# Attention's small matmuls as four 64x64 tiles: operands without zero blocks, two exponentials per pair of heads

## The chip, the cores and the metric

The kernel runs on one core of one Trainium2 chip. A core has a matrix engine (TensorE; PE in the profile, its weight loads PEld), a vector engine (VectorE, DVE), a scalar engine (ScalarE, ACT), GpSimd (POOL) and SyncE (SP), which work side by side and wait for one another through semaphores. POOL and SP also issue most transfers. The metric is the device time of one execution in microseconds, lower is better. Three timed executions of the kernel before gave 365.85 us as their median, from 364.59 to 366.14.

## The reference

Windowed attention with a few global positions, followed by a wide layer with an activation and a second matrix product:

```python
def _attn_ref(q, k, v, global_idx):          # B, H, S, D = 8, 8, 576, 64; 8 global positions
    window = 32
    scores = scale * np.matmul(q, k.transpose(0, 1, 3, 2))
    mask = np.abs(pos[:, None] - pos[None, :]) <= window
    mask = mask | is_global[:, None] | is_global[None, :]
    scores = np.where(mask, scores, -1000000000.0)
    scores = scores - np.max(scores, axis=-1, keepdims=True)
    attn = np.exp(scores)
    attn = attn / (np.sum(attn, axis=-1, keepdims=True) + 1e-09)
    return np.matmul(attn, v).astype(np.float32)

def _moe_ref(x, w_in, w_out, alpha):         # x: 4608 x 512; w_in: 512 x 2048; w_out: 2048 x 512
    h = x @ w_in
    s = np.sin(alpha * h)
    g = h + s * s / (alpha + 1e-09)
    return (g @ w_out).astype(np.float32)
```

## The kernel before

**Attention, one pair of heads at a time.** A batch has eight heads, worked as four pairs (`hp` 0 to 3; the two heads of a pair are `t` 0 and 1). The 576 keys of a head are split into 12 tiles of 48 (`NT12`); each key tile is joined by the 8 global keys. Two key tiles of even and odd number (`i % 2`) hold the even and odd positions of one segment. A key tile meets only 60 columns of even and 60 of odd queries, its window and the global queries, so one score matmul has 120 columns (`WCOL`).

Keys lie in `KX` so that head 0 of a pair has partitions 0 to 63 and columns 0 to 63 of a 128x128 block, head 1 the rest, and the two other 64x64 blocks are zero. One 128x128 matmul per key tile (L742) gives both heads' scores at once: 12 a pair, four into one PSUM tile of the ring `ring` (two buffers), then one exponential on ACT (L750) and one multiplication by `MASK` on DVE (L753) for these four: three of each a pair. Values `VX` have the same block form, and `OB` is a block matrix of ones, which sums the exponentials. `products` (L784) multiplies each key tile's `E` by `VX` (numerator) and by `OB` (denominator); the output columns are split into two halves at `CUT`, each a PSUM bank, and two of the 12 tiles cross the cut: 14 matmuls each, 28 a pair, of 120, 88 or 32 columns. They add up in `zn` (numerator) and `zd` (denominator), two banks each; the last pair has its numerator in `zd` and its denominator in the banks of `zr`, which the ring gives up. Then ACT takes the logarithm of the denominator and the exponential of its negative (L810, L813, the reciprocal), DVE sums the global queries' columns (L794) and multiplies (L816) into `xT`, the input of the wide layer.

**The order of work is written by hand.** `attention` issues, for each pair, the scores of this pair, then the products of the pair before, then reciprocal and normalisation of the pair before. Between them `fill(n)` issues the next n matmuls of `gemm2` of the batch before: the second matrix product, 128x128 by 512 columns (L1049), in blocks of 16 that add up in one of two banks `zo[0]`, `zo[1]`, taken in turn; ACT copies each finished block out (L1055) and SP stores it (L1062). A `gemm2` has four blocks (even batches) or five (odd ones), 64 or 80 matmuls. How many go where is given by START, PER_SCORES, MIDST and, within `gemm1`, PER_GROUP; LATE and GROUP_LATE hold for the first batches.

**gemm1** (L992) makes the hidden layer: 16 groups of 8 matmuls of 288 columns into `zn`, `zr`, `zd` in turn, then Sin on ACT (L1022), the square on ACT or DVE (L1026, L1028) and the sum on DVE into `H2` (L1030). Then the attention of the next batch runs beside `gemm2` of this one. `beside` puts DVE copies of the next keys and queries (L350, L357) between.

**Loads.** POOL issues the value loads (`load_v`, 16 a batch) and writes the global keys and queries (`place_globals`); SP issues the global values (`load_vg`, 8 a batch), the transposes of keys and queries (`turn_qk`) and the stores. At the start `KX`, `QX` and `VX` are cleared by ACT, DVE and POOL. The lines behind L1193 run 54 matmuls on the values and `H2` whose results nobody reads, in 64x64 tiles and whole.

Of the kernel before, what the change touches and what calls it, by code (L numbers as in the profile page):

```python
# [10 lines left out]
ALU = mybir.AluOpType  # L11
AF = mybir.ActivationFunctionType
DT = mybir.dt
# [234 lines left out]
def kernel(  # L248
# [43 lines left out]
    VX = [main.tile([P, NHP, NT12, P], DT.bfloat16, name=f"VX{i}") for i in range(2)]  # L292
    KX = [main.tile([P, NHP, NT12, P], DT.bfloat16, name=f"KX{i}") for i in range(2)]
# [7 lines left out]
    OB = main.tile([P, P], DT.bfloat16, name="OB")  # L301
    MASK = main.tile([P, NT12, WCOL], DT.bfloat16, name="MASK")
# [10 lines left out]
    W2 = main.tile([P, DFF], DT.bfloat16, name="W2")  # L313
    limit = main.tile([P, 1], DT.float32, name="limit")
    EA = main.tile([P, B * NHP * 3], DT.float32, name="EA")
# [29 lines left out]
    def place(b, which, t, y, copy, hps=slice(0, NHP)):  # L345
# [10 lines left out]
        else:  # L356
            copy(  # L357
                out=KX[b % 2][rows, hps, :, t * D + y * 24 : t * D + y * 24 + 24],
# [8 lines left out]
    def place_globals(b):  # L367

        for hp in range(NHP):
            for t in range(2):  # L370
                rows = slice(t * D, (t + 1) * D)
                nc.gpsimd.tensor_copy(
                    out=KX[b % 2][rows, hp, :, t * D + KT : t * D + KT + NG],
                    in_=kTg[rows, hp, None, :, b].to_broadcast([D, NT12, NG]),
                )
# [13 lines left out]
    def load_v(b, hps=range(NHP)):  # L389
        for hp in hps:  # L390
            for t in range(2):
                for y in range(2):
                    r = t * D + y * 24
                    nc.gpsimd.dma_start(  # L394
                        out=VX[b % 2][r : r + 24, hp, :, t * D : t * D + D],
                        in_=v[b, 2 * hp + t].rearrange("(i a y) d -> y a i d", a=24, y=2)[y],
                    )

    def load_vg(b):
        for h in range(H):  # L400
            t = h % 2
            src = VGb[b::B, h * D : (h + 1) * D] if b else VG0[h::H]
            nc.sync.dma_start(
                out=VX[b % 2][t * D + KT : t * D + KT + NG, h // 2, :, t * D : t * D + D],
                in_=src[:, None, :].to_broadcast([NG, NT12, D]),
            )
# [28 lines left out]
    zn, zd = [banks.tile([P, 2, 512], DT.float32, name=name) for name in ("zn", "zd")]  # L435
    zo = [banks.tile([P, 512], DT.float32, name=f"zo{i}") for i in range(2)]

# [800 lines left out]
```

## Time and profile before

| what | value |
|---|---|
| median of three timed runs | 365.85 us |
| profiled execution, its own time | 366.15 us |
| its span, first to last instruction | 364.4 us |
| mean granted TensorE clock | 0.993 of full |
| attention of batch 0, first scores to first matmul of gemm1 | 16.14 to 33.60 us |
| attention of batch 1 | 54.42 to 72.07 us |
| attention of batch 2 | 96.96 to 115.68 us |
| gemm1 of batch 2 (with the START matmuls behind it) | 115.68 to 136.34 us |
| attention of batch 3, gemm1 of batch 3 | 136.34 to 155.06 to 175.35 us |
| gemm1 of batch 7 begins | 311.10 us |

In a profile page "busy" is the time in which an engine has at least one instruction at work; a matmul's duration includes its way through the array, so successive matmuls overlap, and their pace is read from the distance of their starts. "Idle before, releaser" tells how long an engine stood before an instruction and which event let it go on. The costliest groups of the page and some of its waits:

```profile
L1049 PE MATMUL zo<-w_out,H 128*128 128x512 bf16 x576 | 153.7, 379 | 0.0
L750 ACT ACTIVATE E<-ring 128x480 bf16<-128x480 f32 x96 | 54.2, 567 | 22.6 <-PE ring L742 22.2
L753 DVE TENSOR_TENSOR E<-E,MASK 128x480 bf16<-128x480 bf16 x96 | 36.0, 405 | 16.9 <-ACT E L750 15.5
L742 PE MATMUL ring<-QX,KX 128*128 128x120 bf16 x384 | 38.0, 225 | 6.5 <-ACT E L750 3.0
```

Each line is a group: source line, engine, operation, tiles out<-in, shapes and count, then busy microseconds and mean nanoseconds of one, then the engine's idle time before it and what ended it.

### The profile page before, as it was taken

How to read it: one execution, taken by the hardware profiler on the slowest of the kernel's cores; microseconds unless marked ns; L12 is line 12 of the kernel's file. 1: busy time of each engine (PE TensorE's matmuls, PEld its weight loads, DVE VectorE, ACT ScalarE, POOL GpSimd, SP SyncE). 2: the span in 40 equal slices, each digit the busy share in tenths (PEclk: the TensorE clock that was granted, in tenths of full speed). 3: DMA queues.
4: the chain of work that ended last, by engine and by line, in shares of the span. 5: the costliest groups of instructions: out<-in, count | busy, mean ns of one | idle time of the engine just before them, and what ended most of it. 6: DMA issues, size and time to landing. Idle time of an engine off the chain costs nothing. (4 is left out here: it accounts for less than half of the span.)

```text
span 364.4 us, 8575 instructions
## 1 busy us (share of the span) xinstructions
PE 338.4 (93%) x3110; PEld 230.8 (63%) x3110; DVE 283.3 (78%) x623; ACT 293.5 (81%) x566; POOL 139.2 (38%) x246
## 2 busy tenths in 40 slices
PE   2579978999999999999999999999999999999994
PEld 1467656766567666776666766766676766655453
DVE  6776998588988877888888887888788866798661
ACT  7689997886978788887888897979888888878711
POOL 7992686669874702661066304730000000000001
PEclk9999998999999999999999999999999999999999
DMA  7997999999999783989199904647120011000321
GB/s 118 120 171 162 181 146 189 156 168 198 146 237 202 73 123 81 172 89 161 31 158 120 149 29 50 68 50 148 43 59 29 2 31 60 29 3 0 105 70 53
DMA packets 103580, 38.07 MB, mean 104 GB/s; under 512 B 94139, under 2 KB 98251, under 8 KB 103083
## 3 DMA queue, kind: packets, MB, share of 16 engines
q0 software_dynamic: 56640, 18.56, 44.6%
q1 hardware_dynamic: 46890, 18.89, 25.5%
q8 instruction: 26, 0.43, 0.5%
q14 instruction: 24, 0.19, 0.2%
HBM read 37.15 MB, written 17.83 MB: 151 GB/s over the span
## 5 line engine op out<-in xcount | busy, mean ns | idle before, releaser
L1049 PE MATMUL zo<-w_out,H 128*128 128x512 bf16 x576 | 153.7, 379 | 0.0
L992 PEld LDWEIGHTS <-w_in 128*128 128x128 bf16 x1024 | 98.6, 98 | 45.6 <-issue 9.1
L394 POOL DMA_DIRECT2D VX<-in_v_dram x128 | 83.3, 659 | 89.8 <-PE zd L784 62.9
L1049 PEld LDWEIGHTS <-H 128*128 128x128 bf16 x576 | 52.3, 97 | 37.2
L750 ACT ACTIVATE E<-ring 128x480 bf16<-128x480 f32 x96 | 54.2, 567 | 22.6 <-PE ring L742 22.2
L753 DVE TENSOR_TENSOR E<-E,MASK 128x480 bf16<-128x480 bf16 x96 | 36.0, 405 | 16.9 <-ACT E L750 15.5
L1083 POOL DMA_INDIRECT out_dram<-osb,ghalf x1 | 1.1, 1067 | 119.6 <-POOLq L1206 119.6
L1030 DVE SCALAR_TENSOR_TENSOR H<-s,recipT,zn 128x576 bf16<-128x576 bf16 x47 | 38.2, 814 | 10.3 <-ACT s L1026 6.5
L1026 ACT ACTIVATE s<-sb 128x576 bf16<-128x576 bf16 (+1 forms) x62 | 42.7, 689 | 2.0
L742 PE MATMUL ring<-QX,KX 128*128 128x120 bf16 x384 | 38.0, 225 | 6.5 <-ACT E L750 3.0
L742 PEld LDWEIGHTS <-KX 128*128 128x128 bf16 x384 | 29.0, 102 | 22.0 <-issue 8.8
L1022 ACT ACTIVATE sb<-zn,alphaT 128x576 bf16<-128x576 f32 (+1 forms) x47 | 34.7, 739 | 9.8 <-PE zn L992 9.7
L1030 DVE SCALAR_TENSOR_TENSOR H<-s,recipT,zd 128x576 bf16<-128x576 bf16 x39 | 31.7, 814 | 6.5 <-ACT s L1026 4.7
L1030 DVE SCALAR_TENSOR_TENSOR H<-s,recipT,zr 128x576 bf16<-128x576 bf16 x39 | 31.7, 813 | 4.5 <-ACT s L1026 2.4
L1022 ACT ACTIVATE sb<-zd,alphaT 128x576 bf16<-128x576 f32 (+1 forms) x39 | 28.9, 740 | 7.1 <-PE zd L992 5.8
L1028 DVE TENSOR_TENSOR s<-sb 128x576 bf16<-128x576 bf16 (+1 forms) x66 | 30.7, 465 | 4.1 <-ACT sb L1022 3.6
L1022 ACT ACTIVATE sb<-zr,alphaT 128x576 bf16<-128x576 f32 (+1 forms) x39 | 28.9, 740 | 5.6 <-PE zr L992 5.4
L784 PEld LDWEIGHTS <-VX 128*128 128x128 bf16 x448 | 26.6, 100 | 9.4 <-issue 3.5
L1055 ACT COPY osb<-zo 128x512 f32<-128x512 f32 x36 | 20.8, 577 | 11.3 <-PE zo L1049 10.0
L992 PE MATMUL zn<-xlast,w_in 128*128 128x288 bf16 (+1 forms) x192 | 28.8, 289 | 0.3
L992 PE MATMUL zn<-xT,w_in 128*128 128x288 bf16 x184 | 26.9, 286 | 2.3 <-DVE H L1030 0.9
L784 PE MATMUL zn<-E,VX 128*128 128x120 bf16 (+2 forms) x336 | 26.9, 211 | 1.0 <-DVE xlast L816 0.9
(163 smaller groups left out, 492.6 us busy)
## 6 DMA issues: line engine op xcount, KB each, us to landing
VX<-in_v_dram POOLq DMA_DIRECT2D x128, 36.0 KB, 5.4
kd<-in_k_dram POOLq DMA_DIRECT2D x7, 576.0 KB, 7.1
qd<-in_q_dram POOLq DMA_DIRECT2D x7, 576.0 KB, 10.1
w_in<-in_moe_w_in_dram POOLq DMA_DIRECT2D x4, 512.0 KB, 6.0
w_out<-in_moe_w_out_dram POOLq DMA_DIRECT2D x4, 512.0 KB, 7.8
out_dram<-osb SPq DMA_DIRECT2D x8, 256.0 KB
out_dram<-osb SPq DMA_DIRECT2D x8, 224.0 KB
out_dram<-osb SPq DMA_DIRECT2D x8, 192.0 KB
```

The costliest lines, as they stand in the source:

```text
L394: nc.gpsimd.dma_start(out=VX[b % 2][r : r + 24, hp, :, t * D : t * D + D], in_=v[b, 2 * hp + t].rearrange("(i a y) d -> y a i d", a=24, y= ...
L742: nc.tensor.matmul(out=ps[:, e * WCOL : (e + 1) * WCOL], lhsT=kx[:, hp, i, :], rhs=qx[:, hp, :, s0 : s0 + 60], start=True, stop=True, skip ...
L750: nc.scalar.activation(out=Eg, in_=ps[:, 0 : 4 * WCOL], func=AF.Exp, scale=scale, accum_out=EA[:, n : n + 1])
L753: nc.vector.tensor_tensor(out=Eg, in0=Eg, in1=MASK[:, 4 * g : 4 * g + 4, :].rearrange("p i c -> p (i c)"), op=ALU.mult,)
L784: nc.tensor.matmul(out=out_t[:, half, :, a - half * CUT : z - half * CUT], lhsT=OB[:] if key else VXb[:, hp, i, :], rhs=E[:, i, :, a - s0 ...
L992: nc.tensor.matmul(out=h[e][:, 0:W], lhsT=lhsT, rhs=xT[:, c, e, 0:W], start=(c == 0), stop=(c == CT - 1), skip_group_check=True,)
L1022: nc.scalar.activation(out=sb[:, es, 0:W], in_=h[:, :, 0:W], func=AF.Sin, scale=alphaT[:, nt : nt + 1])
L1026: nc.scalar.activation(out=s2[:, :, 0:W], in_=sb[:, :, 0:W], func=AF.Square)
L1028: nc.vector.tensor_tensor(out=s2[:, :, 0:W], in0=sb[:, :, 0:W], in1=sb[:, :, 0:W], op=ALU.mult)
L1030: nc.vector.scalar_tensor_tensor(out=H2[:, nt, r0 : r0 + S].rearrange("p (e c) -> p e c", e=2)[:, es], in0=s2[:, es, 0:HALF], scalar=recip ...
L1049: nc.tensor.matmul(out=ops[:], lhsT=H2[:, nt, blk * P : (blk + 1) * P], rhs=w_out[:, nt, :], start=(nt == 0), stop=(nt == NT - 1),)
L1055: nc.scalar.copy(out=osb[:], in_=ops[:])
```

## The change

Keys, values, the exponentials `E` and the mask lose their zero blocks. A key tile is now 64 columns wide with the two heads on the two halves of the partitions; `E` and the mask hold even key tiles on partitions 0 to 63 and odd ones on 64 to 127; `OB` goes, and 64 columns of `ones` take its place. Every matmul of the attention works on 64 rows and 64 columns: for scores, the head picks the rows of the array and the parity of the key tile its columns; for products, the parity picks the rows and the head the columns. There are twice as many matmuls, 24 for scores and 56 for products a pair, issued in rounds over the four tiles.

The two row halves are kept in different PSUM banks. Products therefore run in two parts, `crossed` 0 and 1, with `nc.tensor.drain()` between. The scores of a pair go, 8 key tiles of each head, into the two banks of `zr` (now a fixed tile), with one exponential over 960 columns; the remaining third, four of 120 columns, goes into one bank, `zd` for pair 0 and otherwise a `zo` bank that `pick()` chooses, written half before and half after the drain, with a second exponential over 480 columns. `gemm2` also takes its banks from `pick()`. All scores of a pair, its `fill` in one stretch and all products of the pair before now follow one another; the matmul counts for `fill` are 3 at the start, 14 a pair, 4, and 9 within gemm1. `load_vg` issues 12 loads a batch, `place_globals` writes four key pieces instead of eight, the clearing of `KX` and `VX` halves, and the unread matmuls at the end go. Set-up code for mask and places follows the new layout (not shown).

```diff
-    VX = [main.tile([P, NHP, NT12, P], DT.bfloat16, name=f"VX{i}") for i in range(2)]
-    KX = [main.tile([P, NHP, NT12, P], DT.bfloat16, name=f"KX{i}") for i in range(2)]
+    VX = [main.tile([P, NHP, 2, NT12 // 2, D], DT.bfloat16, name=f"VX{i}") for i in range(2)]
+    KX = [main.tile([P, NHP, NT12, D], DT.bfloat16, name=f"KX{i}") for i in range(2)]
...
+    zr = banks.tile([P, 2, 512], DT.float32, name="zr")
     zo = [banks.tile([P, 512], DT.float32, name=f"zo{i}") for i in range(2)]
+    used, opened, clock = [0, 0], [], [0]
+
+    def pick():
+        return min((i for i in range(2) if i not in opened), key=lambda i: used[i])
+
+    def use(i):
+        clock[0] += 1
+        used[i] = clock[0]
+        return zo[i]
...
+        def slot(t, g, u):
+            return 8 + 2 * t + u if g == 2 else 4 * t + 2 * g + u
+
+        def score(hp, g, u, t, z, c):
+            for r in range(2):
+                i = 2 * (g + 3 * u) + r
+                s0 = PAD + begin(i)
+                nc.tensor.matmul(
+                    out=z[r * D : (r + 1) * D, c * WCOL : (c + 1) * WCOL],
+                    lhsT=kx[t * D : (t + 1) * D, hp, i, :],
+                    rhs=qx[t * D : (t + 1) * D, hp, :, s0 : s0 + 60],
+                    start=True, stop=True, skip_group_check=True,
+                )
+
+        def scores(hp):
+            Es[hp] = pairp.tile([P, NT12, WCOL], DT.bfloat16, name="E")
+            for c in range(4):
+                for t in range(2):
+                    score(hp, c // 2, c % 2, t, zr[:, t, :], c)
+
+        def scores_last(hp, t, z):
+            for u in range(2):
+                score(hp, 2, u, t, z, 2 * t + u)
+
+        def expo(hp, n, z):
+            at = (b * NHP + hp) * 2 + n
             nc.scalar.activation(
-                out=Eg, in_=ps[:, 0 : 4 * WCOL], func=AF.Exp, scale=scale, accum_out=EA[:, n : n + 1]
-            )
+                out=Es[hp][:, 8:] if n else Es[hp][:, 0:8].rearrange("p (t i) c -> p t (i c)", t=2),
+                in_=z[:, 0 : 4 * WCOL].rearrange("p (i c) -> p i c", c=WCOL) if n else z[:, :, 0 : 4 * WCOL],
+                func=AF.Exp, scale=scale, accum_out=EA[:, at : at + 1],
+            )
...
+        def product(hp, key, g, crossed):
+            out_t = nd(hp, key)
+            for u in range(2):
+                for r in range(2):
+                    half = r ^ crossed
+                    v = u ^ half
+                    i = 2 * (g + 3 * v) + r
+                    if half not in parts_of(i):
+                        continue
+                    a, z = parts_of(i)[half]
+                    s0 = begin(i)
+                    rows = slice(r * D, (r + 1) * D)
+                    for t in range(2):
+                        bank = (hp, key, half, t)
+                        E = Es[hp][rows, slot(t, g, v)].rearrange("p (x c) -> p x c", x=2)
+                        nc.tensor.matmul(
+                            out=out_t[t * D : (t + 1) * D, half, :, a - half * CUT : z - half * CUT],
+                            lhsT=ones[rows, 0:D] if key else VXb[rows, hp, t, g + 3 * v, :],
+                            rhs=E[:, :, a - s0 : z - s0],
+                            start=bank not in begun, stop=True, skip_group_check=True,
+                        )
+                        begun.add(bank)
+
+        def products(hp, crossed):
+            for key in (1, 0):
+                for g in range(3):
+                    product(hp, key, g, crossed)
...
+        def scores_products(hp, third):
+            scores_last(hp, 0, third)
+            if hp:
+                products(hp - 1, 0)
+            nc.tensor.drain()
+            scores_last(hp, 1, third)
+            if hp:
+                products(hp - 1, 1)
...
+            n_start, n_fill = (START, PER_PAIR) if b > 1 else (0, LATE)
+            fill(n_start)
+            beside(-1)
+            for hp in range(NHP):
+                third = use(pick())[:] if hp else zd[:, 0, :]
+                scores(hp)
+                scores_products(hp, third)
+                expo(hp, 0, zr)
+                mask(hp, 0)
+                if hp:
+                    invert(hp - 1)
+                expo(hp, 1, third)
+                if hp:
+                    normalise(hp - 1)
+                mask(hp, 1)
                 if wide and hp == last:
                     keep_globals(slice(0, last))
+                fill(n_fill[hp])
+                if b == 1 and hp < 2:
+                    idle()
+                beside(hp)
+        products(last, 0)
+        nc.tensor.drain()
+        products(last, 1)
         inverse(last)
         nc.scalar.preload_act_table(AF.Sin)
         sums(last, 1)
         fill(MIDST)
-        products(last, range(3), (0,))
         sums(last, 0)
...
     def gemm2(b):
         lo, hi = (0, 4) if b % 2 == 0 else (4, 9)
         for blk in range(lo, hi):
-            ops = zo[(blk + b // 2) % 2]
+            z = pick()
+            opened.append(z)
+            ops = use(z)
             for nt in range(NT):
...
             nc.scalar.copy(out=osb[:], in_=ops[:])
+            opened.clear()
+            use(z)
...
-    START = 2
-    PER_SCORES = ((1, 11, 3), (3, 3, 4), (3, 3, 4), (3, 4, 5))
-
-    LATE = ((0, 0, 0), (0, 0, 0), (2, 3, 3), (4, 4, 6))
+    START = 3
+    PER_PAIR = (14, 14, 14, 14)
+
+    LATE = (0, 0, 8, 14)
     MIDST = 4
-    PER_GROUP = (0, 0, 5) + 11 * (1,) + (0, 0)
+    PER_GROUP = (0, 0, 5, 0, 1, 0, 0, 1, 0, 0, 1, 0, 1, 0, 0, 0)
```

`inverse` is the logarithm and the exponential of its negative; `invert(hp)` is `inverse` and the two `sums`. For batch 0 a separate order without `fill` uses `zd`, `zr` and the two `zo` banks in turn for the last third.

236 lines of the change are left out of this document (99 added, 137 removed).

## The prediction

> **What bounds the kernel now.** I read the page first, then the engines' busy time stretch by stretch, then the timeline of one attention stage and of the last microseconds, and the list of waits. The profiled execution took 366.15 us, its span 364.4 us, so 1.75 us lie around the span; the median of the runs shown is 365.85 us, 0.3 us below. The sum is made against 366.15 and 0.3 is taken off at the end.
>
> ```profile
> span 364.4 us, 8575 instructions
> PE 338.4 (93%) x3110; PEld 230.8 (63%) x3110; DVE 283.3 (78%) x623; ACT 293.5 (81%) x566; POOL 139.2 (38%) x246
> ```
>
> An average says little about stages, so here are one attention stage (136 to 155 us) and the first matrix product after it (155 to 175 us); the columns are the stretch, its length, then the busy time of PE, PEld, DVE, ACT and POOL.
>
> ```profile
> 136.34:155.06 18.72, 18.71 (x213) 12.51 (x213) 15.07 (x35) 16.20 (x41) 8.12 (x13) 1.00 0.72 128
> 155.06:175.35 20.29, 20.02 (x150) 14.21 (x148) 16.89 (x29) 16.94 (x27) 6.93 (x15) 1.00 0.91 111
> ```
>
> The reader is to see that PE is idle for 0.01 us of the one and 0.27 us of the other, at a granted clock of 1.00, while ACT and DVE have 2 to 4 us to spare. Six such cycles (attention of batches 2 to 7 with the first products behind them) run at about 39 us each. In them only TensorE's own time and new waits of TensorE count; fewer exponentials are worth nothing while matmuls hide ACT (without that cover one of 0.55 us a pair would go, less what the longer one takes more).
>
> **What one pair of heads costs now.** The timeline of that stage:
>
> ```profile
> 136.98 2.53 PE L1049 MATMUL zo<-w_out,H 128*128 128x512 bf16 x11
> ...
> 141.93 0.36 PE L784 MATMUL zn<-E,VX 128*128 128x88 bf16 x4
> ...
> 142.79 0.37 PE L742 MATMUL ring<-QX,KX 128*128 128x120 bf16 x4
> ...
> 143.00 0.36 PE L784 MATMUL zn<-E,VX 128*128 128x120 bf16 x4
> ...
> 143.39 1.03 PE L1049 MATMUL zo<-w_out,H 128*128 128x512 bf16 x4
> 143.66 0.19 ACT L750 ACTIVATION_READ_ACCUMULATOR E<-ring 128x1 f32 x1
> 143.76 0.73 ACT L810 ACTIVATE L<-zd,tiny 128x576 f32<-128x576 f32 x1
> ```
>
> Starts tell pace. Four score matmuls take 143.00-142.79 = 0.21 us, 0.0525 each. The 28 products of a pair take (142.79-141.93)+(143.39-143.00) = 1.25 us. A pair is 3x0.21+1.25 = 1.88 us, a stage 4x1.88 = 7.52 us. A second-product matmul takes (2.53-0.38)/10 = 0.215 us, 0.38 being the length of a lone one; its 72 a cycle do not change.
>
> **What tiles cost.** The kernel before ends with matmuls in 64x64 tiles (L1199), so the trace prices them:
>
> ```profile
> 354.28 1.46 PE L1049 MATMUL zo<-w_out,H 128*128 128x512 bf16 x6
> 355.66 1.06 PE L1076 MATMUL zo<-w_out,HG 128*64 128x256 bf16 x16
> ...
> 357.91 0.54 PE L1199 MATMUL zd<-H,VX 64*64 64x120 bf16 x24
> 358.24 0.79 PE L1199 MATMUL zn<-H,VX 64*64 64x120 bf16 x24
> 358.96 0.49 PE L1199 MATMUL zd<-H,VX 128*128 128x120 bf16 x6
> ```
>
> The first 24 go round all four tiles: six rounds in 358.24-357.91 = 0.33 us, 0.055 a round with the start, so four tiles do cost what one whole matmul costs (0.0525). A change between whole array and tiles: the last 512-column matmul starts at 354.28+5x0.215 = 355.36 and would make room at 355.57, and the next kind starts at 355.66: 0.09 us. The next 24 go two by two, twelve rounds in 358.96-358.24-0.09 = 0.63, 0.0525 each again.
>
> Now the changed stage, from the diff. Scores: a pair has four rounds of four tiles into zr and, for the third part, two rounds of two tiles on each side of the drain: 8x0.0525 = 0.42, a stage 1.68. Products: for each of numerator and denominator a tile gets four matmuls before the drain and three after, of 120, 88 or 32 columns. No tile matmul in the trace is narrower than 120; if width counted, as it does in the whole array (1.25 us for 28), a pair is 0.60, if each is a full round 14x0.0525 = 0.735. I take 0.735, the row with tiles: 2.94 a stage. The Trainium skill (TensorEngine Tiling (Array Packing), Restrictions) has column tiles lose the fast weight load; the trace has 107 ns for a 64-wide load against 98 for a whole one, and by the rule the 0.735 would hold, by width 0.5 us a stage less. Changes of mode: two a pair and two for the last pair's products, 10x0.09 = 0.9. Drains: five a stage, and none stands in this stage of the trace. Below, a drain is an emptied array, 0.09. Above, it is the last matmul's 0.21, a weight load of 0.10, and the 28 matmuls behind it at 0.028 each (54 loads of L1199 in 1.52 us) in place of eight rounds, 0.78-0.42 = 0.36: 0.67. I take 0.30, the last matmul's end and the load, since a drain waits for the one and keeps the other from being fetched ahead: 1.5. Sum 1.68+2.94+0.9+1.5 = 7.02, so tiles gain 0.5 us a stage, 3.0 in six.
>
> **Waits that the change adds.** (a) The third part of the scores now goes to whichever zo bank the second product has not open, and the next block of the second product, 16 matmuls long, takes just that bank, because pick() returns the one used longest ago. That block then stands behind the pair's second exponential, which is queued on ACT behind logarithm and reciprocal of the pair before. From the products' last start: 0.1 to the logarithm, 0.76 to the next,
>
> ```profile
> 144.52 0.68 ACT L813 ACTIVATE R<-L 128x576 f32<-128x576 f32 x1
> ...
> 145.20 0.55 ACT L750 ACTIVATE E<-ring 128x480 bf16<-128x480 f32 x1
> ```
>
> 0.68 to the exponential, 0.57 for it: 2.1 us. The fill of 14 starts 0.14 after the products; a block that begins after its matmul number o waits 2.1-0.14-0.215o. Counting START 3, 14 a pair, MIDST 4, 9 in the first product against blocks of 16: with 80 matmuls to place (attention of batches 2, 4, 6) blocks begin at o=13 of pair 0, 1 of pair 2 and 3 of pair 3; with 64 (3, 5, 7) at 5 of pair 0, 7 of pair 1, 9 of pair 2, 11 of pair 3. Pair 0 uses zd, so nothing there waits for an exponential. Waits 1.75+1.32 and 0.45+0.02. After o=13 the bank's copy (0.58) is also late for the third part of pair 1: its block's last matmul lands 0.96 with the copy after its start, PE is there at 2x0.215+0.09+0.21 = 0.73, 0.23. Together 3.3 and 0.47, for three of each 11.3 us. PE works in order, so scores, products and the fill behind it all move. (b) Pair 0's third part goes to zd, where group 14 of the first product lies until
>
> ```profile
> 136.46 0.81 DVE L1030 SCALAR_TENSOR_TENSOR H<-s,recipT,zd 128x576 bf16<-128x576 bf16 x1 [0.29 <-ACT s L1026]
> ```
>
> 137.27. After the last first-product matmul (the fill starts at 135.91) PE needs 3x0.215+0.09+0.21 and would be there at 136.86: 0.41. Seven fewer fill matmuls in that stage let DVE and ACT trail it more; I take 0.6, bounds 0 and 1: 3.6 in six.
>
> **Parts at nothing.** Batch 0 and 1 wait for chains on ACT and DVE: fewer exponentials (four of 0.55 a batch) against masks and products that now wait for a longer exponential with no fill; 0, bounds -1.5 and +1.5. Setup is shorter by one clearing of 1.34 on DVE and part of the mask, but the queries' copies on DVE hold the first scores, -0.3 inside that bound. Four KX copies fewer on POOL before batch 1 would start its scores 1.6 earlier, but the table load ends at 55.12 and the first exponential starts at 55.14 already. SP gets 12 loads of global values a batch for 8, which took 5.76 us in the setup (0.72 each): 2.9 us more on its queue, ahead of the turning of the next keys and the stores; they are issued before a first product of 20 us, which covers it. POOL's value loads stay 16 a batch. The probe L1199 runs beside the last output's transfer and is worth nothing.
>
> **Sum.** -3.0+11.3+3.6 = +11.9: 366.15+11.9 = 378.05, less 0.3: 378.
>
> **Rivals.** *Cheap drains and no bank waits (faster):* place, pairs 1 to 3; the second exponential is done before the block needs its bank, that is within 0.36 us of the products in pair 2. For it: ACT has 2.5 us to spare in the stage. Against it: the order of ACT's queue. Then 11.3 goes; a drain of 0.09 gives 6x1.05 = 6.3 and narrow products 6x0.5 = 3.0: 357. Without bank waits it turns from slower to faster once a drain is under 0.28. *No bank waits, drains as taken:* 366.5. *Issue sets the pace:* tiles double the attention matmuls to 80 a pair; at 0.028 each 2.24 instead of 1.155, 4.3 a stage, 26 in all: 404. For it: 54 loads in 1.52 us, never tried for longer; against it, rounds of 0.0525 are four at 0.013. The Trainium skill (TensorE: Matmul & The Clock Gate, "Wait — 56ns, not 53.3ns?") has the sequencer spend about 62 ns on a matmul with hardware decoding off; an estimate by it is 4.96 us a pair and some 470 us. The trace starts 48 tile matmuls in 1.05 us, 22 ns each, which speaks against it as far as so short a run can. *Tiles do not run side by side:* 80x0.0525 a pair, 73 us more, 451; the rounds of L1199 speak against it.
>
> **Chances.** Forecast 0.60, own range 370 to 389 (drains 0.09 to 0.67 are -6.3 and +11, half the bank waits -5.6). Faster rival 0.17, no bank waits 0.12, issue 0.08, one by one 0.03. Within 0.5%, which is 364.0 to 367.7, is what a measurement cannot tell from no change: 0.07 of the third case and 0.01 of others, so 0.08; faster 0.19, slower 0.73. Range 358 to 391: it leaves out half of the faster rival and the two slow ones.
>
> **What would show it.** Right: idle of TensorE before the second product's first matmul of a block, released by the exponential, near 1.7 us in pair 2 of the 80s; idle before the third part of pair 0 released by DVE's H; gaps of about 0.35 from start to start at drains; rounds of 0.0525. Wrong: blocks that begin without idle, drains under 0.15, or stretches of tiles slower than four in 0.06.

## The result, and the profile after

The changed kernel takes 404.6 us (median of four runs, 402.5 to 408.2), the kernel before beside it 366.0 us: a ratio of 1.1075, with a 95% interval from 1.0985 to 1.1164. Slower was forecast; the 378 us and the range up to 391 were too low. The profiled execution is the longest of the four, 408.2 us. Its page begins so:

```profile
span 406.5 us, 10957 instructions
PE 341.2 (84%) x4330; PEld 208.9 (51%) x4330; DVE 279.6 (69%) x586; ACT 288.4 (71%) x502; POOL 123.2 (30%) x219
```

TensorE's busy time hardly moved (338.4 us before), its share fell from 93 to 84%: it now waits. Between the starts of the stages (first scores of a batch to its first matmul of gemm1, and on to the next scores) the 42 us lie here:

| stretch of the profiled execution | before | after | more |
|---|---|---|---|
| start to first scores of batch 2 | 97.0 | 111.4 | 14.4 |
| attention of batch 2 and gemm1 of batch 2 | 39.4 | 51.0 | 11.6 |
| attention of batch 3 to attention of batch 7 | 174.8 | 192.4 | 17.6 |
| gemm1 of batch 7 to the end | 53.3 | 51.8 | -1.5 |

Below: attention of batch 3, gemm1 of batch 3, attention and gemm1 of batch 4, with the columns of the same view before (stretch, length, busy PE, PEld, DVE, ACT, POOL).

```profile
162.32:183.17 20.85, 19.74 (x382) 10.52 (x382) 14.56 (x31) 15.35 (x33) 9.03 (x15) 1.00 0.77 117
183.17:203.70 20.53, 19.51 (x142) 13.53 (x140) 17.13 (x31) 17.39 (x26) 4.29 (x10) 1.00 0.52 86
203.70:227.47 23.77, 19.96 (x382) 10.64 (x382) 14.55 (x31) 15.29 (x33) 11.06 (x21) 1.00 0.76 114
227.47:248.00 20.53, 19.50 (x141) 13.53 (x139) 17.22 (x31) 17.88 (x27) 2.08 (x4) 1.00 0.49 84
```

Attention grew from 18.72 to 20.85 us (batch 3) and from 18.7 to 23.77 (batch 4). gemm1 did not shrink (20.29 before), though six matmuls of the second product had been moved out of it and TensorE is idle for a whole microsecond of it. The timeline of TensorE in the attention of batch 4:

```profile
203.70 0.40 PE L757 MATMUL zr<-QX,KX 64*64 64x120 bf16 x16
204.25 0.67 PE L757 MATMUL zd<-QX,KX 64*64 64x120 bf16 x8
204.85 3.19 PE L1126 MATMUL zo<-w_out,H 128*128 128x512 bf16 x14
...
212.92 0.40 PE L757 MATMUL zr<-QX,KX 64*64 64x120 bf16 x16
...
213.42 0.35 PE L828 MATMUL zn<-E,VX 64*64 64x120 bf16 x16
213.89 0.24 PE L757 MATMUL zo<-QX,KX 64*64 64x120 bf16 x2
...
214.41 0.39 PE L1126 MATMUL zo<-w_out,H 128*128 128x512 bf16 x1
216.51 2.97 PE L1126 MATMUL zo<-w_out,H 128*128 128x512 bf16 x13 [1.72 <-ACT E L779]
...
220.90 0.82 PE L1126 MATMUL zo<-w_out,H 128*128 128x512 bf16 x3
223.01 2.53 PE L1126 MATMUL zo<-w_out,H 128*128 128x512 bf16 x11 [1.29 <-ACT E L779]
```

The small matmuls of a whole pair, scores and products, go from 212.92 to 214.41: 1.49 us, where the same work took 1.88. The last product before the drain starts at 213.59, the first matmul behind it at 213.89: 0.30 from start to start. Then, one matmul and three matmuls into the fill, TensorE stands for 1.72 and 1.29 us before a new block of the second product: the bank waits of the prediction (1.75 and 1.32), at the predicted matmuls.

The first row of the table, and some 6 us of the second (an even batch is about 5 us longer in any case), have other reasons. SP's queue and GpSimd at the start, before:

```profile
15.88 5.76 SPq L403 DMA_DIRECT2D VX<-VG  x8
32.26 2.16 SPq L340 DMA_TRANSPOSE kt<-kd  x1
36.46 0.33 POOL L1127 COPY seen<-kt 1x1 bf16<-1x1 bf16 x1 [6.90 <-DMA kt<-kd]
49.92 0.63 POOL L696 CAST VGb<-H 64x512 bf16<-64x512 f32 x1
```

and after:

```profile
15.88 11.23 SPq L404 DMA_DIRECT2D VX<-VG  x16
38.09 2.04 SPq L340 DMA_TRANSPOSE kt<-kd  x1
42.37 0.18 POOL L1206 COPY seen<-kt 1x1 bf16<-1x1 bf16 x1 [13.78 <-DMA kt<-kd]
55.53 0.67 POOL L710 CAST VGb<-H 64x512 bf16<-64x512 f32 x1
```

Batch 0 has sixteen loads of global values for eight (each head twice, once for each half of the partitions). They hold up the queries and then the key transposes on SP by 5.8 us. GpSimd waits for those transposes in its own order (a one-element copy stands ahead of its next loads), so w_in, the values of batch 1, w_out and the table `VGb` all come 5.6 us later. And in the attention of batch 2, from the timeline of all engines, in order of time:

```profile
105.97 0.53 POOL L331 DMA_DIRECT2D kd<-in_k_dram  x1
106.26 10.36 SPq L340 DMA_TRANSPOSE kt<-kd  x1
116.73 5.81 SPq L340 DMA_TRANSPOSE qt<-qd  x1
122.73 0.92 DVE L357 COPY KX<-kt 64x1152 bf16<-64x1152 bf16 x2 [6.67 <-DMA kt<-kd]
124.53 0.31 PE L828 MATMUL zd<-E,ones 64*64 64x88 bf16 x10 [3.78 <-DVE GS L844]
```

The transposes of batch 3's keys and queries start together with the casts of batch 4 (L331, DRAM to DRAM) and take 10.4 and 5.8 us, where before they took 4.4 and 3.9 and had ended when those casts were issued (101.33 us). DVE's placing of these keys stands ahead of the masks of this batch, so the products wait.

### The profile page after: what moved, and what is told of

Read it like the earlier page. It is cut to its first block, busy times and chain, and to the rows that moved or that the text cites. A ratio compares the mean times of both kernels' runs of the same rounds, so it can differ in the third digit from the quotient of the medians.

```text
span 406.5 us, 10957 instructions
## 1 busy us (share of the span) xinstructions
PE 341.2 (84%) x4330; PEld 208.9 (51%) x4330; DVE 279.6 (69%) x586; ACT 288.4 (71%) x502; POOL 123.2 (30%) x219
## 3 DMA queue, kind: packets, MB, share of 16 engines
q1 hardware_dynamic: 47178, 18.89, 22.7%
## 5 line engine op out<-in xcount | busy, mean ns | idle before, releaser
L1126 PE MATMUL zo<-w_out,H 128*128 128x512 bf16 x576 | 143.9, 386 | 10.2 <-ACT E L779 10.2
L1126 PEld LDWEIGHTS <-H 128*128 128x128 bf16 x576 | 54.3, 99 | 69.8 <-issue 17.6
L788 DVE TENSOR_TENSOR E<-E,MASK 128x960 bf16<-128x960 bf16 x64 | 33.2, 529 | 33.0 <-ACT E L779 32.5
L779 ACT ACTIVATE E<-zr 128x960 bf16<-128x960 f32 (+1 forms) x33 | 31.6, 957 | 31.7 <-PE zr L757 31.7
L757 PEld LDWEIGHTS <-KX 64*64 64x64 bf16 x768 | 18.3, 112 | 31.6 <-issue 30.8
L1132 ACT COPY osb<-zo 128x512 f32<-128x512 f32 x36 | 20.9, 580 | 11.6 <-PE zo L1126 9.1
L828 PE MATMUL zd<-E,ones 64*64 64x120 bf16 (+2 forms) x672 | 23.8, 224 | 6.4 <-DVE GS L844 3.8
L828 PE MATMUL zn<-E,VX 64*64 64x120 bf16 (+2 forms) x672 | 22.3, 224 | 7.5 <-DMA VX<-VGb 4.5
L860 ACT ACTIVATE L<-zd,tiny 128x576 f32<-128x576 f32 x24 | 17.8, 741 | 14.2 <-PE zd L828 13.7
```

Source lines behind the costliest of these rows:

```text
L757: nc.tensor.matmul(out=z[r * D : (r + 1) * D, c * WCOL : (c + 1) * WCOL], lhsT=kx[t * D : (t + 1) * D, hp, i, :], rhs=qx[t * D : (t + 1) * ...
L779: nc.scalar.activation(out=Es[hp][:, 8:] if n else Es[hp][:, 0:8].rearrange("p (t i) c -> p t (i c)", t=2), in_=z[:, 0 : 4 * WCOL].rearran ...
L788: nc.vector.tensor_tensor(out=Em, in0=Em, in1=MASK[:, 2 * n : 2 * n + m // 2].rearrange("p g u c -> p (g u c)")[:, None].to_broadcast([P, ...
L828: nc.tensor.matmul(out=out_t[t * D : (t + 1) * D, half, :, a - half * CUT : z - half * CUT], lhsT=ones[rows, 0:D] if key else VXb[rows, hp ...
L1126: nc.tensor.matmul(out=ops[:], lhsT=H2[:, nt, blk * P : (blk + 1) * P], rhs=w_out[:, nt, :], start=(nt == 0), stop=(nt == NT - 1),)
L1132: nc.scalar.copy(out=osb[:], in_=ops[:])
```

## Experiments

Each was run beside the kernel before (366.2 to 366.7 us). "A2 at" is the first score of batch 2 in the profiled execution, "A2" the length of its attention, "A3-A7" the stretch of the table above.

| kernel | us, median | ratio to before, 95% | A2 at | A2 | A3-A7 |
|---|---|---|---|---|---|
| before | 366.0 | | 97.0 | 18.7 | 174.8 |
| the change | 404.6 | 1.1075 (1.0985 to 1.1164) | 111.4 | 30.4 | 192.4 |
| second exponential first | 396.5 | 1.0815 (1.0672 to 1.0958) | 112.3 | 25.9 | 185.8 |
| the same, and old spread in gemm1 | 390.6 | 1.0655 (1.0594 to 1.0715) | 112.1 | 20.5 | 182.1 |
| no global value loads | 399.3 and 420.6 | | 102.2 | 50.8 | 192.5 |
| global values by rows, batch 1 on | 400.3 | 1.0918 (1.0886 to 1.0950) | 109.4 | 23.5 | 192.7 |
| late casts | 406.2 | 1.1087 (1.1053 to 1.1120) | 111.7 | 25.0 | 193.9 |
| before, casts early | 368.0 and 388.5 | | 96.5 | 40.0 | 175.0 |
| all four, batch 0 by rows behind the queries | 389.4 | 1.0638 (1.0595 to 1.0680) | 112.8 | 19.3 | 182.5 |
| the same, first third in zo | 404.3 | 1.1034 (1.0987 to 1.1082) | 113.9 | 24.2 | 190.7 |
| all four, batch 0 as in the change | 390.9 | 1.0656 (1.0619 to 1.0693) | 110.0 | 22.7 | 183.1 |
| the same, START 4 | 389.0 | 1.0634 (1.0565 to 1.0703) | 109.3 | 20.2 | 180.5 |
| as two rows above, 32 more drains | 395.4 | 1.0789 (1.0746 to 1.0832) | 112.0 | 21.1 | 187.0 |
| START 4, 22 more idle matmuls | 387.4 | 1.0551 (1.0506 to 1.0595) | 113.1 | 19.0 | 180.0 |
| the change, batch 0 by rows, early | 401.6 | 1.0964 (1.0918 to 1.1010) | 106.6 | 26.2 | 194.7 |
| START 4 and batch 0 by rows, early | 380.7 | 1.0396 (1.0355 to 1.0438) | 106.7 | 18.8 | 180.7 |

### The cycles

*The second exponential ahead of the logarithm.*

```diff
+                expo(hp, 1, third)
                 if hp:
                     invert(hp - 1)
-                expo(hp, 1, third)
-                if hp:
                     normalise(hp - 1)
```

> Only the order on ACT changes, for batches from 1: the second exponential is issued ahead of the logarithm and the reciprocal of the pair before. Theory: the waits of TensorE before a new block of the second product (1.72 and 1.29 us in pairs 2 and 3 of batch 4) are that exponential, queued 1.45 us behind the other two; it is now done about 0.5 us after the products, so the waits fall under 0.4 us, some 2.5 us an even batch and 0.4 an odd one: about 396 us. Rival: the block waits for something else that ends at the same time (the copy out of the bank, or the masks of the pair): no change, 403 us or more.

TensorE's waits from the attention of batch 3 to the end of that of batch 7, total, times and longest, in the change:

```profile
PE zo L1126 <- ACT E L779: 7.3, 7, 1.7
```

and with this edit:

```profile
PE zo L1125 <- ACT E L779: 1.1, 2, 0.6
```

396.5 us, where 396 was expected: the bank waits go from 7.3 to 1.1 us in these five stages, the stretch loses 6.6, the kernel 8. The order of ACT's queue, not a lack of ACT's time, made that wait.

*In addition, START, PER_PAIR and PER_GROUP near the old spread.*

```diff
-    START = 3
-    PER_PAIR = (14, 14, 14, 14)
+    START = 2
+    PER_PAIR = (13, 12, 12, 12)
...
-    PER_GROUP = (0, 0, 5, 0, 1, 0, 0, 1, 0, 0, 1, 0, 1, 0, 0, 0)
+    PER_GROUP = (0, 0, 5) + 11 * (1,) + (0, 0)
```

> The order of the run with the second exponential first, and the second product's matmuls spread as before the change: 2 at the start, 13, 12, 12, 12 a pair, 4, and 16 within the first product (in the change 3, 14 a pair, 4, and 9). Theory: the first product's stage keeps its 20.5 us with 9 fill matmuls as with 16, because Sin, squares and sums on ACT and DVE set its end, so the 7 matmuls moved into the attention stage are paid twice; with them back the attention stages shorten by about 1.9 us each and the first product stays at 20.2 to 20.7: 1.6 us a cycle, 8 us less than the run with the exponential first alone. Rival: TensorE's work is only moved: the first product's stage grows by 1.5 us and the time is the same within 2 us.

390.6 us, 6 less (8 expected), 3.8 of it in the stretch from batch 3 to 7. Six or seven matmuls went back from each attention to gemm1, which goes from 20.2 to 20.7 up to 20.4 to 21.2 us; attention falls to 19.6 to 20.1. So gemm1 grew by 0.3 us on average, not by the 1.3 that six matmuls take on TensorE: most of their time had been given away in the move. The reason stands in gemm1's own timeline; in the change, with a fill behind every second or third group:

```profile
193.63 1.14 PE L1068 MATMUL zd<-xlast,w_in 128*128 128x288 bf16 x8
194.61 1.14 PE L1068 MATMUL zn<-xlast,w_in 128*128 128x288 bf16 x8
195.90 1.14 PE L1068 MATMUL zr<-xlast,w_in 128*128 128x288 bf16 x8
196.87 0.38 PE L1126 MATMUL zo<-w_out,H 128*128 128x512 bf16 x1
```

Eight matmuls need 0.98 us from start to start (193.63 to 194.61), but the next group comes 1.29 later. Before, with a fill in each:

```profile
166.79 1.14 PE L992 MATMUL zn<-xlast,w_in 128*128 128x288 bf16 x8
167.77 0.38 PE L1049 MATMUL zo<-w_out,H 128*128 128x512 bf16 x1
167.98 1.14 PE L992 MATMUL zr<-xlast,w_in 128*128 128x288 bf16 x8
```

the distance is 1.19, which is TensorE's own time for a group and one fill. Over twelve groups of the change (187.61 to 201.98 us) the mean is 1.20 all the same. What sets it is the way of a group through its bank:

```profile
187.61 1.14 PE L1068 MATMUL zn<-xlast,w_in 128*128 128x288 bf16 x8 [0.25 <-DVE H L1106]
188.79 0.74 ACT L1098 ACTIVATE sb<-zn,alphaT 128x576 bf16<-128x576 f32 x1 [0.95 <-PE zn L1068]
189.56 0.68 ACT L1102 ACTIVATE s<-sb 128x576 bf16<-128x576 bf16 x1
190.28 0.81 DVE L1106 SCALAR_TENSOR_TENSOR H<-s,recipT,zn 128x576 bf16<-128x576 bf16 x1 [0.71 <-ACT s L1102]
191.15 1.14 PE L1068 MATMUL zn<-xlast,w_in 128*128 128x288 bf16 x8 [0.22 <-DVE H L1106]
```

Matmuls, Sin, square and sum follow one another, and the next group gets `zn` 3.54 us after the last one did. Three tiles taken in turn make that 1.18 us a group, although ACT and DVE both stand idle in between (0.95 and 0.71 us). One fill a group fits beside it (0.98 and 0.2155 are 1.20): it had been free.

*Where the first pair's last third lies.* Two kernels with all mends (the two above, row loads, late casts); the one with the third in `zo`:

```diff
-                third = use(pick())[:] if hp else zd[:, 0, :]
+                third = use(pick())[:]
```

> The kernel with every mended part together, and the third part of the first pair's scores in the free bank of the second product and no longer in zd. Theory: the wait of 0.6 us for zd at the first pair goes in six stages, and the kernel is 3 us faster than the same without it, near 384. Rival: another wait takes its place (the second product's next block behind this pair's exponential, or VectorE, which trails by as much in the first product), and the time stays within 1 us, near 387.

The rival, and far more of it: 404.3 against 389.4 us, 8.2 of them from batch 3 to 7. Its timeline shows what took the place of a wait of 0.6 us:

```profile
202.69 0.38 PE L1130 MATMUL zo<-w_out,H 128*128 128x512 bf16 x1 [2.75 <-ACT E L779]
```

The next block needs the bank in which that third lies, and waits for the first pair's second exponential.

*Four fill matmuls ahead of the first pair, eleven behind it.*

> The same kernel as the one before it in this call, with four matmuls of the second product ahead of the first pair and eleven behind it, in place of two and thirteen: 0.43 us more cover before the third part of the first pair needs zd; the blocks of the second product begin where they did. Theory: the wait for VectorE's H on zd (0.5 us in these stages) goes and 2 to 3 us of the whole, near 378. Rival: the exponentials of the pair start 0.43 us later and a later wait (for the second exponential, or for VectorE in the first product) takes the gain, within 1 us of the kernel without it.

In the stretch from batch 3 to 7 TensorE's wait for DVE at `zd` falls from 2.7 us in five times to 0.2 in one, and the stretch from 183.1 to 180.5: the theory's 2.6 us. The kernel does not come near 378: the medians, 390.9 and 389.0, differ by less than the runs scatter (385.8 to 392.1).

*One drain more a pair.*

```diff
+            nc.tensor.drain()
             scores_last(hp, 0, third)
```

> The same kernel as the first of this call, with one drain more in every pair, between the first two thirds of the scores and the last third: 32 more, 24 of them in the six stages in which TensorE sets the time. Theory: a drain costs 0.25 us there beyond the matmul's own 0.05 (0.28 to 0.30 from start to start), so these 24 cost 6 us, and all 32 between 6 and 8. Rival: a drain is all but free where the next matmuls would have waited anyway, under 2 us.

395.4 against 390.9: 4.5 us for 32 drains, 3.9 for the 20 in the stretch, 0.19 each. Neither free nor the full 0.25.

### The first three batches

*No global value loads at all* (the values of the global positions are left out of the products).

```diff
     def load_vg(b):
+        return
```

> Leaves out the loads of the global values into VX (load_vg issues nothing; those rows stay zero). Theory: the first three attention stages are long (22.96, 26.02 and 30.41 us against 17.46, 17.65 and 18.72 before) because SP's queue now carries 16 such loads for batch 0 and 12 for the others at 0.66 us each: products wait for them, the transposes of the next keys go out late behind them, and TensorE falls to the half clock while it waits. Then the three stages come back to about 18, 18.5 and 23.5 us (the last keeps its bank waits), 19 us less: about 385 us. Rival: these stages are long because tiles, drains and the single pair of exponentials have no second-product matmuls beside them to hide their chain; then the waits only change their name and the time stays over 398 us.

Batch 2 starts 9.2 us earlier (102.2 us), as the theory has it: attention of batch 0 goes from 23.0 to 19.3, of batch 1 from 26.0 to 21.1 us. But the two runs took 399.3 and 420.6 us, and in the profiled one, the longer, the transposes of batch 3 met the casts again and took 15.1 and 27.0 us.

*Row loads for batch 1 and later.* A copy of `VGb` with each head's row six times (DVE, once), then two transfers a batch for twelve.

> The change with the global values of batches 1 to 7 loaded by 2 transfers of whole rows of 6 KB a partition instead of 12 of 128 B pieces, from a copy that DVE makes once (64 partitions x 3072) in the first product of batch 0; batch 0 keeps its 16 loads. Theory of SP's queue: the stage of batch 1 loses its waits for global values (4.5 us), and the transposes of the keys come some 8 us earlier, so the stage of batch 2 loses its 6.7 us wait of DVE: about 390 us. Rival (number of loads does not matter, only the bytes or the products' own chain): over 400 us.

400.3 us, 4 less than the change, not the 15 of the theory. Batch 2 starts at 109.4 us, 2 earlier, so these loads make only a small part of the lateness.

*The casts of batch 4 behind batch 4's first value loads.*

```diff
-            if b < 3:
-                cast_qk(b + 2)
+            if b == 1:
+                cast_qk(3)
             load_v(b + 2, (0,))
+            if b == 2:
+                cast_qk(4)
```

> The changed kernel, in which GpSimd issues the casts of batch 4 behind the first value loads of batch 4 and no longer ahead of them, so that they go out some 20 us later. Theory: in the changed kernel the key transposes of batch 3 took 10.4 and 5.8 us because these two casts met them; alone they take 2 to 5 us each, VectorE no longer waits 6.7 us for the keys in the attention of batch 2, that stage falls from 30.4 to about 23.8 us, and the kernel from 404.6 to about 398. Rival: the transposes are late because SP's queue issues twelve loads ahead of them; then the stage stays at 30 us and the kernel at 404.

The transposes take 2.7 and 2.8 us and that stage falls by 5.4 us of the 6.6 expected; the kernel does not (406.2 us, where 398 was expected). The profiled run of the change was its longest, and its three others, not profiled, took 402.5 to 405.8: how much of a collision they had can't be said, and the median shows no gain.

*The kernel before, with the casts of batch 4 early* (`cast_qk(4)` ahead of `place_globals(3)`).

> The kernel before, with one edit: GpSimd issues the casts of batch 4 ahead of its copies of the global keys of batch 3 and no longer behind them, some 4 to 6 us earlier. Theory: then they meet the key transposes of batch 3 (92 to 101 us) here too; the transposes take over 8 us, the attention of batch 2 grows from 18.7 us by 3 to 20 us, and the kernel takes 369 to 386 us. Rival, by which copies and casts have no part in it: 366 us as before, transposes of 4 us each.

368.0 and 388.5 us. The profiled run is the long one:

```profile
91.70 8.38 SPq L340 DMA_TRANSPOSE kt<-kd  x1
92.65 0.53 POOL L331 DMA_DIRECT2D kd<-in_k_dram  x1
93.17 0.53 POOL L331 DMA_DIRECT2D qd<-in_q_dram  x1
100.18 22.43 SPq L340 DMA_TRANSPOSE qt<-qd  x1
122.38 0.93 DVE L357 COPY KX<-kt 64x1152 bf16<-64x1152 bf16 x2 [20.12 <-DMA kt<-kd]
```

In this execution the old kernel, moved by one edit into the collision, loses 21.3 us in the attention of batch 2 (40.0 for 18.7) and 1 us elsewhere; the other one, 368.0 us, has no profile. So the collision is no property of the tiles, and its price varies much from one execution to the next.

What brings the change into it can be read from the two timelines. Counted from the start of gemm1 of batch 1, the transposes start at 20.0 us before and at 21.2 in the change, the casts of batch 4 at 29.3 and at 20.9. From the casts of batch 3 to those of batch 4 GpSimd needs 22.6 us before and 20.6 in the change: two rounds of copies of global keys are 4.4 us shorter (four for eight, 1.2 us for 3.4), and 2.0 of that are left. The other 6.4 of the 8.4 us were there at the casts of batch 3, since the attention of batch 1 had made TensorE late by more than GpSimd was.

*All four mends, batch 0 by rows too,* the loads issued behind the eight transfers of queries.

> The changed kernel with every mended part together: the second exponential ahead of the logarithm, the old spread of the second product's matmuls over the groups of the first, the global values of batch 1 and later by two transfers of whole rows, those of batch 0 by two transfers too (from a copy that VectorE makes late in the setup), and the casts of batch 4 behind the value loads. Theory: the 390.6 us of the first two mends fall by 1.5 us in the attention of batch 0 and by 2 to 3 us in that of batch 1, to about 387; cycles of attention and first product stay near 40.5 us, 1.5 us above the kernel before, and the kernel before is not reached. Rival: the loads of batches 0 and 1 are covered once the rest is mended, 390 to 391.

389.4 us, between the two. The loads of batch 0 landed late:

```profile
PE zn L828 <- DMA VX<-VG0r: 10.1, 1, 10.1
```

The attention of batch 0 took 30.0 us, that of batch 1 only 21.0.

*The same with batch 0's sixteen loads back.*

> The kernel with every mended part together, but the sixteen global value loads of batch 0 as in the changed kernel, since the two loads that replaced them were issued behind eight transfers of queries and made the products of the attention of batch 0 wait 10.1 us. Theory: that stage falls from 30.0 to about 22 us, the rest stays, 381 us. Rival: the lateness only moves into the attention of batch 1, as in the kernel with the first two mends alone (26.5 us there), 387 to 390.

390.9 us, the rival: batch 0 is 7.7 us shorter, batches 1 and 2 are 4.3 and 3.4 longer. So the end of batch 1 seems to be set by something other than these loads.

*22 matmuls into TensorE's idle time around batch 1.*

> The kernel with four matmuls ahead of the first pair, with 22 more matmuls of 512 columns whose results nobody reads: eight into zn ahead of the last group of the first product of batch 0 (TensorE idles there for VectorE), and eight instead of one behind each of the first two pairs of the attention of batch 1. In all kernels so far the attention of batch 1 was the longer the longer the granted clock stayed at one half around it: 17.7 us with 3.4 us of half clock, 21.0 to 21.6 with 10.2, 24.5 to 26.0 with 13.7, 25.3 to 26.5 with 17.1. Theory: the half clock follows TensorE's idle time and then lengthens the stage itself; with the idle time filled it falls to 3.4 to 7 us, the stage from 24.6 to about 21.5 to 22.5 us, the kernel by 2 to 3 us to about 386. Rival: the half clock goes with the stage's waits and costs nothing of its own; then the clock rises but the stage stays at 24 to 25 us, or it gets longer because the scores stand behind the added matmuls.

The half clock fell only from 13.7 to 10.2 us, in three pieces, and the attention of batch 1 grew from 24.6 to 27.1. With the same 10.2 us the kernel above (batch 0 by rows behind the queries) needs 21.0: the half clock alone doesn't set the length of this stage. The median (387.4 us) is within the scatter of the runs around 389.0.

*Batch 0 by rows, issued early.* In the change alone, and with all mends and START 4:

```diff
-            for h in range(H):
-                for at in rows:
-                    nc.sync.dma_start(
-                        out=VX[0][at, h // 2, h % 2], in_=VG0[h::H][:, None, :].to_broadcast([NG, NT12 // 2, D])
-                    )
+            nc.vector.tensor_copy(out=VG0r[:], in_=VG0[:, None, :].to_broadcast([NG * H, NT12 // 2, D]))
+            for at in rows:
+                nc.sync.dma_start(
+                    out=VX[0][at].rearrange("p h t i d -> p (h t) (i d)"), in_=VG0r[:].rearrange("p i d -> p (i d)")
+                )
```

> The changed kernel with one edit: the sixteen global value loads of batch 0 become two, from a copy that VectorE spreads out late in the setup, issued ahead of the eight transfers of queries; the 24 loads of batches 1 and 2 stay. Theory: eight loads more on SP's queue put the key transposes of batch 1 from 32.3 to 38.1 us, GpSimd waits for these in order (13.8 us for 6.9), and everything behind it (two thirds of w_in, the values of batch 1, w_out, the table of global values: 49.9 to 55.5 us) comes 5.7 us late into the attention of batch 1. With two loads the transposes start at 30 to 32 us, that table is cast at about 50, the attention of batch 2 starts at 103 to 106 us instead of 111.4, and the kernel takes 396 to 399 us. Rival: the start of the attention of batch 2 is set by the loads of batches 1 and 2 or by TensorE's half clock; then it stays at 109 us or later and the kernel above 401.

> The kernel with all mends (second exponential first, old spread over the groups, row loads from batch 1 on, late casts, four matmuls ahead of the first pair) and the two early loads of batch 0. Theory: the start of the attention of batch 2 falls from 109 us to 99 to 103, and the kernel from 389 to 379 to 382 us, which leaves the cycles (40 to 41 for 39.0 us) as what keeps it above the kernel before. Rival: the end of the attention of batch 1, which stood at 83 to 88 us in every variant that kept loads of global values, stays there; 387 to 389 us.

In the change alone:

```profile
16.45 1.33 SPq L405 DMA_DIRECT2D VX<-VG0r  x2
31.11 2.49 SPq L341 DMA_TRANSPOSE kt<-kd  x1
50.66 0.65 POOL L711 CAST VGb<-H 64x512 bf16<-64x512 f32 x1
```

Transposes and table are back at the times of before (32.26 and 49.92), and batch 2 starts 4.8 us earlier, at 106.6 us (103 to 106 expected, 109 by the rival). The kernel took 401.6 us, 3 less and not the 396 to 399 expected; transposes of 8.8 us met the casts in that profile. With everything together, 380.7 us, inside the 379 to 382 expected, but not in the way of the theory: batch 2 starts at 106.7 and not at 99 to 103. Against START 4 (389.0 us) that is 2.6 us earlier, and its attention is 1.4 us shorter in the profiles; the rest of the 8.3 us between the medians has no account. It is the best of these kernels, and 4% above the kernel before.

## Why the prediction was wrong, step by step

**Tiles: right.** A pair was put at 1.64 us with its drain and two changes of mode and takes 1.49 plus 0.09 for entering. A change of mode was put at 0.09: the score matmul at 212.92 starts 0.31 behind a 512-column matmul of 0.216. The drain was added at 0.30; it shows 0.28 to 0.30 from start to start, where a round takes 0.05, and one more a pair cost 0.19. Pair 0 takes 1.15 us with a wait of 0.34, the last products 1.12. So a stage's small matmuls take 0.81+3x1.49+1.12+5x0.09 = 6.85 us for 7.52, 0.7 saved (0.5 predicted). The rivals with the sequencer and with tiles one by one are out: the 80 tile matmuls of a pair take 1.49 us, 19 ns each, drain included. The Trainium skill (TensorE: Matmul & The Clock Gate, "Wait — 56ns, not 53.3ns?") has starts never nearer than about 25 ns; the trace does not agree for tiles. That 404 is the time of the issue rival is chance.

**Bank waits (a): right in place and size.** 8.0 us predicted for batches 3 to 7, 7.3 measured; moving the exponential took them away.

**The wait for zd (b): right in place, too large.** 0.6 us a stage was taken, 0.34 shows in the attention of batch 4.

**The moved matmuls: the step that failed in the cycles.** The prediction read that "ACT and DVE have 2 to 4 us to spare", concluded that "In them only TensorE's own time and new waits of TensorE count", and took the second product's matmuls as a sum: "its 72 a cycle do not change". It counted "START 3, 14 a pair, MIDST 4, 9 in the first product" to place the blocks, and of their move it said only that "Seven fewer fill matmuls in that stage let DVE and ACT trail it more; I take 0.6, bounds 0 and 1". But attention went from 51 fills to 60, 9x0.2155 = 1.9 us, and gemm1, paced at 1.2 us a group by the way through a bank, gave nothing back. ACT and DVE do have time to spare, and a chain that runs through both sets the pace all the same. In even batches -0.7 for the tiles, 1.9 for the moved matmuls, 3.0 of bank waits and 0.65 for `zd` and the copied bank make 4.9 (5.1 measured); in odd ones, with 0.4 of bank waits and 0.34 for `zd`, 1.9 (1.9 to 2.3 measured). Two even and three odd attentions, with 1.2 us in the four stages of gemm1, are the 17.6 us from batch 3 to 7, for 8.5 predicted. The sentence that seven fewer let the others trail had the cause in it; it priced one wait instead of asking what sets gemm1 once TensorE has a microsecond to spare.

**"Parts at nothing": the larger error.** Batches 0 and 1 were put at 0 (-1.5 to +1.5) and came out 14.4 us longer. Two sentences failed. "SP gets 12 loads of global values a batch for 8" overlooked that batch 0 has sixteen and that these stand ahead of the transposes for which GpSimd waits; "they are issued before a first product of 20 us, which covers it" named a cover, but not who waits on SP's queue behind them. That the loads are at fault for 9.2 of the 14.4 us is shown (so much earlier without any; 4.8 with batch 0's alone mended). What keeps the attention of batch 1 at 24 us with few and early loads (17.7 before) is known in part, and from rows alone. In the best kernel TensorE's waits in it add up to 6.3 us for 3.2 before (the longest: masks and exponentials 2.2, the values by rows 1.6, `zd` 1.3), and the fills that fall into the half clock start 0.42 us apart for 0.2155, which is 1.5 us over seven of them. That is 4.6 of the 6.5 us by which this stage is longer (24.2 for 17.7).

**"Four KX copies fewer on POOL": weighed for the wrong thing.** They were weighed as a gain of 1.6 us, which does not come; that the casts come earlier against the transposes was not asked. Of the 8.4 us by which they do, the traces put 2.0 down to the copies and the rest to the lateness of batch 1; no run changed the copies alone. That the transposes get long when they meet the casts is shown in both kernels; in the median of the change no part of the time is shown to be the collision's.

**What the mends account for.** Of 38.6 us between the medians, the exponential's place takes back 8.1 (6.6 from batch 3 to 7), the spread in gemm1 5.9 (3.8), and all mends together 23.9; row loads and late casts added nothing to the first two as long as batch 0 had its sixteen loads (390.9 us for 390.6). The profile of the best kernel is 15.1 us longer than the one before: 9.7 us at the start of batch 2, 0.3 in batch 2 and 6 from batch 3 to 7, less 0.9 in the tail. In that stretch attention has the 51 fills of before again and is up to 0.3 us longer all the same, gemm1 (with two START matmuls more, 0.43 us) 0.7 to 1.8. In the START 4 kernel, whose stretch is as long, the small matmuls of a stage take 7.2 to 7.9 us, for 6.7 to 7.1 in the change and 7.6 before: what the tiles save is gone again. Its trace names masks of DVE ahead of the last products (0.07 and 0.18 us idle in batches 4 and 5) and once the second exponential ahead of a block (0.46); the rest was not followed.

## What to carry to other kernels

Work that fills another engine's pace is free where it stands and costs its full time where it is moved to: before a fill is moved, ask what sets the pace of the stage that it leaves. It need not be a busy engine: here it was a chain through three tiles, with every engine in it idle for a part of the time. When a buffer is shared between two streams, follow the order of the queue that frees it; here one exponential two places too late cost 8 us. And count what every edit adds to each issuing queue, batch by batch, and who waits behind it on that queue: eight small loads more in batch 0 made everything behind them late by nearly 6 us.

## What the runs showed of the hardware

- Transposes on SP's queue mostly took 1.9 to 5.9 us. Where two casts from DRAM to DRAM were issued within 2.5 us of one, the longer of the batch's two took 8.3 to 27.0 us: in seven profiles (10.4 in the change, 10.4 with the second exponential first, 8.3 with the old spread too, 27.0 without loads, 8.7 with rows from batch 1 on, 8.8 with batch 0 by rows early, 22.4 in the old kernel with early casts). In the nine others the longest took 5.6.
- In the pair at 212.92 us the 64x64 tiles of a round start 1 to 10 ns apart and a round of four about every 0.05 us; a drain between them shows 0.28 to 0.30 us from start to start but cost 0.19 in time when one more was added to each pair.
- Sixteen transfers to 8 partitions each took SP 11.2 us to issue; two with the same bytes took 1.3 us.
- TensorE's granted clock fell to one half for 3.4 us or multiples of it: near batch 1 from 55.7 to 59.1 us before and from 64.1 to 77.8 in the change. In the 3.4 us ahead of the fall TensorE was busy for 1.30 us before and 2.02 us in the change; with 1.69 of 3.41 us from 214.3 in the change the clock stayed full. So the busy time of one such stretch doesn't tell whether the clock will fall.
